# Sliding-window attention and SwiGLU: the output projection on four 64x64 TensorE tiles, with the row sums of a token group in one place

## The chip, the cores and the metric

The kernel runs on one core of a Trainium2 chip. The time is the device time of one execution in microseconds (us), the median of several runs; lower is better. A core has five engines that run their own instruction queues and wait for one another by semaphores: TensorE (PE in the profile, with its weight loads in a row of their own, PEld), VectorE (DVE), ScalarE (ACT), GpSimd (POOL) and SyncE (SP, which here only issues DMAs). Matmul results land in PSUM, which has 8 banks of 128 partitions by 512 floats.

## The reference, cut to what matters

```python
# q, k, v: (8 batches, 8 heads, 576 positions, 64)
scores = q @ k^T / sqrt(64)                      # only 0 <= i - j < 64 is kept
attn   = exp(scores - max) / sum(exp(scores - max))
x      = (attn @ v) laid out as 4608 tokens x 512
out    = (silu(x @ w_gate) * (x @ w_val)) @ w_out   # 512 -> 1536 -> 512
```

Inputs and output are float32; the kernel multiplies in bfloat16 and adds up in float32.

## The kernel before, in words

The 4608 tokens go through in nine groups of 512 (`NT` = 9, index `t`). Groups 0 to 6 and 8 are the first 512 positions of a batch each; group `LAST` = 7 gathers the last 64 positions of all eight batches. The order of all instructions is written out by hand (`tc.manual_schedule()`): each engine executes its own in the order in which the code issues them, and semaphore waits are put in where an instruction touches a tile that another engine has written or read.

For each group there are two stages.

*The attention visit.* `scores(t, w)` (L269) multiplies keys by queries for four of the eight heads, `w` = 0 or 1. Head size and window are 64, so these matmuls use 64 rows and 64 columns of the 128x128 array, and four of them, on four quarters of the array, run side by side. ACT takes the exponential out of PSUM (L282), DVE multiplies by the window's mask (L285) and adds the two blocks that share columns into `both` (L290). `sums` lets TensorE add up `both` (`totals`, L302, four 64x64x512 matmuls per `w`), and ACT makes the reciprocal of the total as exp(-log) (`log` L316, `invert` L319). `mix` (L386) multiplies the weights by the values, and `scale` (L402, DVE) multiplies the result by the reciprocal: that is `xT[t]`, the 512 tokens with the features on the partitions.

*The gate.* For each of 12 blocks `m` of 128 hidden features, `gate_value` (L448) makes g (4 matmuls of 128x128x512 with `wg`) and v (4 with `wv`) in two PSUM banks. `gate_end` lets ACT take the Silu of g (L441) and DVE multiply it by v into `hT[t][:, m]` (L442). After some blocks (`turns`) DVE transposes a quarter of the queries and keys of group t + 1 (`turn`: L207, L217), and for 3 <= t < 7 a quarter of the extra keys for `LAST` after block 8 (`turn_k`).

The output projection of group t - 1 (`project`, L457: for each of four token blocks `s` of 128, 12 matmuls of 128x128x512 over the hidden features) is put into the attention visit of group t, between scores, sums and mix, so that TensorE has work while ACT and DVE work on the softmax. `project_end` copies the PSUM result to SBUF (`os_`, L464) and SP stores it. Groups 0 and 1 meet in a visit written out by hand (L713 to L738), and the last group's projection stands at the end, its last part split in columns (`project_last`, L499). Before all that a prologue (L515 to L668) loads, casts and transposes group 0 on TensorE, and computes its attention.

PSUM: `two[0]` and `two[1]` are tiles of two banks each; `bank[4]` to `bank[7]` are tiles of one bank each. Scores and mix use `two`; g and the projection alternate between banks 4 and 5 (`out_tile`), v and the sums between banks 6 and 7 (`d_tile`); only group 1's sums use `two` (`sums_wide`).

In the loop over groups a visit reads:

```python
            set_exp()                       # ACT's table for exp and log
            scores(t, 0)
            project(t - 1, 0)
            ...
            project_part(t - 1, (1,), (o_ps,), range(5))
            scores(t, 1)
            sums(t, 0)
            project_part(t - 1, (1,), (o_ps,), range(5, 12))
            project_end(t - 1, 1, o_ps)
            project(t - 1, 2)
            sums(t, 1)
            mix_all(t)
            project(t - 1, 3)
        set_silu()                          # ACT's table for Silu
```

Loads for group t + 2 are issued by POOL (queries, keys) and SP (values) after the visit of t; nothing in their code is touched.

Of the kernel before, what the change touches and what calls it, by code (L numbers as in the profile page):

```python
# [17 lines left out]
def kernel(  # L18
# [23 lines left out]
    fsb = ctx.enter_context(tc.tile_pool(name="fsb", bufs=3))  # L42
    hpool = ctx.enter_context(tc.tile_pool(name="hpool", bufs=2))
    ps = ctx.enter_context(tc.tile_pool(name="ps", bufs=1, space=PSUM))
    two = [ps.tile([P, 2, 512], FP32, name=f"two{i}") for i in range(2)]
    bank = [two[i][:, j] for i in range(2) for j in range(2)]
    bank += [ps.tile([P, 512], FP32, name=f"one{i}")[:] for i in range(4)]

    wg = cst.tile([P, 4, DFF], BF16, name="wg")
    wv = cst.tile([P, 4, DFF], BF16, name="wv")  # L50
# [198 lines left out]
    def half(x):  # L249
        return slice(64 * x, 64 * x + 64)  # L250

    def scores(t, w):

        qT = queries[t]
        s_ps = wide(), wide()
        for j in range(8):
            if t == LAST:
                k_j = kT[t % 2 if j < 4 else 2]
                pieces = [(j, j + 1, 0, k_j, P * (j % 4) + 64),
                          (j, j + 1, 1, k_j, P * (j % 4))]  # L260
            else:
                pieces = [(j, min(8, j + 2), 0, kT[t % 2], 64 * j)]
            for lo, hi, c, src, k0 in pieces:
                for h in range(2):
                    for x in range(2):
                        slot = s_ps[h][half(x)].rearrange("r a b -> r (a b)")
                        n = hi - lo
                        o = P * j + 64 * c
                        nc.tensor.matmul(  # L269
                            slot[:, o:o + 64 * n].rearrange(  # L270
                                "r (n e y) -> r e n y", n=n, e=16
                            ),
                            src[half(h), 2 * w + x, k0:k0 + 64],
                            blocks(qT[half(h), 2 * w + x], t, lo, hi).rearrange(
                                "r e (n y) -> r e n y", n=n
                            ),
                        )
        n = 1024 if t == LAST else 960
        for h in range(2):
            E = eb[2 * w + h]  # L280
            flat = E[:].rearrange("r s z -> r (s z)")[:, 64:64 + n]
            nc.scalar.activation(  # L282
                flat, s_ps[h][:].rearrange("r a b -> r (a b)")[:, 0:n], AF.Exp, scale=0.125
            )
# [5 lines left out]
            nc.vector.tensor_add(both[:], E[:, 1:17:2], E[:, lo:lo + 15:2])  # L290
            weights[t, w, h] = E, both
# [7 lines left out]
    def totals(t, w, d):  # L299
        for h in range(2):  # L300
            for x in range(2):
                nc.tensor.matmul(  # L302
                    d[x][half(h)].rearrange("r (e j y) -> r j e y", e=16, j=8),
                    ones[half(x), 0:D],
                    weights[t, w, h][1][half(x)].rearrange("r j (e y) -> r j e y", e=16),
                )
# [11 lines left out]
    def invert(r):  # L318
        nc.scalar.activation(r, r, AF.Exp, scale=-1.0)  # L319

    def sums(t, w):
        d = d_tile(), d_tile()
        totals(t, w, d)
        for x in range(2):
            r = room(1)[:, 0]
            if t == NT - 1:
                log(r.rearrange("r (x e) -> r x e", e=16), turned(d[x]))
            else:
                log(r, d[x])
            invert(r)  # L330
            inverse[t, 2 * w + x] = r

    def sums_wide(t):
        rs = room(2), room(2)
        tiles = wide(), wide()
        for w in range(2):
            totals(t, w, (tiles[w][:, 0], tiles[w][:, 1]))
            for x in range(2):
                inverse[t, 2 * w + x] = rs[w][:, x]
        for w in range(2):  # L340
            log(rs[w], tiles[w][:])
        for w in range(2):
            invert(rs[w])

# [24 lines left out]
                    start=m == 0, stop=m == 7,  # L369
                )  # L370

    def marker(b, x):
        nc.tensor.matmul(bank[b][0:D, 0:16], ones[half(x), 0:D], ones[half(x), 0:16])

    def mix(t, w, o):
        E = [weights.pop((t, w, h))[0] for h in range(2)]
# [24 lines left out]
            r = r.rearrange("r (x e) -> r x e", e=16)  # L401
        nc.vector.tensor_mul(x, o_ps, r)  # L402

    taken = {"a": 0, "g": 0, "v": 0}

    def take(tag):
        taken[tag] += 1
        return taken[tag] % 2 ^ 1

    def wide():  # L410
        return two[take("a")]

    def d_tile():
        return bank[6 + take("v")]

    def mix_all(t):
        tiles = wide(), wide()
        for w in range(2):
            mix(t, w, (tiles[w][:, 0], tiles[w][:, 1]))
        for u in range(4):  # L420
            scale(t, u, tiles[u // 2][:, u % 2])

    def gate_one(t, m, ps, w, c):
        nc.tensor.matmul(  # L424
# [17 lines left out]
        nc.vector.tensor_mul(hT[t][:, m, :], sg[:], v_ps[:])  # L442

    def gate_value(t, m):
        pair = gate_tiles()
        for ps, w in zip(pair, (wg, wv)):
            for c in range(4):
                nc.tensor.matmul(  # L448
                    ps[:], w[:, c, P * m:P * m + P], xT[t][:, c, :],
                    start=(c == 0), stop=(c == 3),  # L450
                )
        gate_end(t, m, pair)

    def project_part(t, ss, tiles, cs):
        for c in cs:
            for s, o_ps in zip(ss, tiles):
                nc.tensor.matmul(  # L457
                    o_ps[:], hT[t][:, c, P * s:P * s + P], wo[:, c, :],
                    start=(c == 0), stop=(c == 11),
                )  # L460
# [24 lines left out]
    def out_tile():  # L485
        return bank[4 + take("g")]

    def project(t, s):
        o_ps = out_tile()
        project_part(t, (s,), (o_ps,), range(12))  # L490
        project_end(t, s, o_ps)

    def project_last(t, s):
        r0 = S * batch(t) + P * s
        os_ = fsb.tile([P, 512], FP32, name="os_", tag="os_", bufs=4)
        for f0, f1 in ((0, 384), (384, 512)):
            o_ps = out_tile()
# [149 lines left out]
    part_first((0, 1), 0, (1, 5))  # L647
    part_first((0, 1), 1, (6, 4))
    part_first((2,), 1, (2, 6, 4))
    marker(7, 1)  # L650
# [5 lines left out]
    marker(7, 0)  # L656
    for u in range(3):
        part_first((u,), 0, (0, 2, 4, 6), 6 if u < 2 else None)
    scale(0, 0, bank[aos[0]])
# [55 lines left out]
    for u in (2, 3):  # L715
        turn_q(1, u)
    scores(1, 0)
    tiles = [out_tile(), d_tile(), out_tile(), d_tile()]

    def columns(c0, c1, s0=0, s1=4):  # L720
        project_part(0, range(s0, s1), tiles[s0:s1], range(c0, c1))

    columns(0, 2, 0, 2)
    columns(0, 2, 2, 4)
    columns(2, 3)
    scores(1, 1)
    columns(3, 7)
    sums_wide(1)
    load_qk(2)
    load_halves(nc.gpsimd, vb[0], 2)  # L730
    columns(7, 9)
    columns(9, 10, 0, 2)
    mix_all(1)
    columns(9, 10, 2, 4)
    columns(10, 12, 0, 2)
    columns(10, 12, 2, 4)
    for s in range(4):
        project_end(0, s, tiles[s], on_a if s < 2 else on_v)  # L738

    for t in range(1, NT):  # L740
        if t > 1:
            set_exp()
            scores(t, 0)
            project(t - 1, 0)
            if t == 2:
                stage_v(3)
            o_ps = out_tile()
# [62 lines left out]
```

## Time and profile before

| | |
|---|---|
| median of 3 runs | 324.94 us (324.93 to 325.21) |
| span of the profiled execution, first to last instruction | 322.4 us |
| time of the profiled execution itself | not given beside its span; median less span is 2.5 us |
| PE busy | 317.1 us, 98% |
| DVE, ACT, POOL busy | 219.5, 166.8, 145.8 us |
| mean granted TensorE clock | 0.999 |
| gate matmuls (L448) | 832 of 128x128x512 |
| projection matmuls (L457, L499) | 420 of 128x128x512, 24 narrower |

How to read it: a busy time counts the time in which at least one instruction of the engine runs. Matmuls overlap, so a matmul that lasts 0.379 us by its row starts 0.216 us after the one before it. In the timeline a row stands for several equal instructions in a row: start, length, engine, line, operation, what it writes and reads, how many, and in brackets how long the engine was idle before and what ended that. Line numbers are those of the kernel before.

### The profile page before, as it was taken

To read this page: it belongs to the slowest core of one execution; us is meant where nothing else is said; L and a number is where in the kernel's file an instruction comes from. 1 tells how busy PE (TensorE), PEld (TensorE's weight loads), DVE (VectorE), ACT (ScalarE), POOL (GpSimd) and SP (SyncE) were. 2 spreads that over 40 slices of the span, in tenths; PEclk is the share of its full clock that TensorE was granted. 3 is DMA by queue.
4 is the path that set the end of the run, shared out by engine and by line. 5 is a ranking of instruction groups with operands and counts; after the bars stand their busy time and mean duration, and the time that the engine had idled before them with its cause. 6 is when DMAs were issued, how large, how long until landed. Compare 5 with 4: busy or idle time off the path is not lost.

```text
span 322.4 us, 7047 instructions
## 1 busy us (share of the span) xinstructions
PE 317.1 (98%) x2774; PEld 150.5 (47%) x2774; DVE 219.5 (68%) x349; ACT 166.8 (52%) x239; POOL 145.8 (45%) x259
## 2 busy tenths in 40 slices
PE   7999999999999999999999999999999999999995
PEld 3644444444544444444444544454444544444443
DVE  5866846597676867777688766876696586773432
ACT  5954665356633763368335833665347533773310
POOL 4955656966075795586125989462200000000000
PEclk9999999999999999999999999999999999999999
DMA  7999999999989999949903999799401400020012
GB/s 252 202 197 198 206 142 223 150 158 126 199 162 198 114 166 195 195 74 226 198 11 46 170 163 97 57 211 179 87 3 35 100 2 0 14 86 36 0 28 103
DMA packets 83521, 40.35 MB, mean 125 GB/s; under 512 B 64160, under 2 KB 78752, under 8 KB 83488
## 3 DMA queue, kind: packets, MB, share of 16 engines
q0 software_dynamic: 51488, 22.59, 58.3%
q1 hardware_dynamic: 31456, 16.79, 21.0%
q10 hardware_dynamic: 544, 0.52, 0.5%
q8 instruction: 21, 0.34, 0.4%
q14 instruction: 12, 0.10, 0.1%
HBM read 53.02 MB, written 9.44 MB: 194 GB/s over the span
## 4 chain that ended last, share of the span: by engine, by line
PE 95%; DMA 2%; DVE 1%; SPq 1%; issue 0%; DVEq 0%
PE one L448 56%; PE one L457 29%; PE two L269 3%; PE two L386 2%; DMA k_f<-in_k_dram 2%; PE one L424 2%; PE one L302 1%; PE one L499 1%; SPq L77 1%; PE two L424 1%; DVE kT L198 0%; PE two L702 0%; PE one L351 0%; DVE qT L573 0%; PE two L302 0%
## 5 line engine op out<-in xcount | busy, mean ns | idle before, releaser
L441 ACT ACTIVATE sg<-one 128x512 f32<-128x512 f32 x107 | 63.9, 597 | 113.6 <-PE one L448 86.7
L442 DVE TENSOR_TENSOR hT<-sg,one 128x512 bf16<-128x512 f32 x107 | 74.2, 694 | 61.9 <-PE one L448 57.8
L448 PE MATMUL one<-xT,wg 128*128 128x512 bf16 x416 | 106.8, 379 | 0.0
L448 PE MATMUL one<-xT,wv 128*128 128x512 bf16 x416 | 106.8, 379 | 0.0
L457 PE MATMUL one<-wo,hT 128*128 128x512 bf16 x420 | 95.2, 380 | 0.0
L126 POOL DMA_DIRECT2D k_s<-in_k_dram x112 | 60.8, 552 | 29.0 <-DMA q_s<-in_q_dram 21.8
L448 PEld LDWEIGHTS <-wv 128*128 128x128 bf16 x416 | 40.7, 98 | 49.1
L448 PEld LDWEIGHTS <-wg 128*128 128x128 bf16 x416 | 40.5, 98 | 48.8
L457 PEld LDWEIGHTS <-hT 128*128 128x128 bf16 x420 | 39.0, 98 | 46.7 <-issue 2.0
L282 ACT ACTIVATE eb<-two 128x960 bf16<-128x960 f32 (+1 forms) x32 | 29.5, 975 | 15.1 <-PE two L269 15.0
L217 DVE STREAM_TRANSPOSE kT<-k_s 128x512 bf16<-128x512 bf16 x28 | 36.1, 1289 | 0.0
L285 DVE TENSOR_TENSOR eb<-eb,mask 128x960 bf16<-128x960 bf16 (+1 forms) x32 | 21.1, 658 | 11.5 <-ACT eb L282 11.5
L402 DVE TENSOR_TENSOR xT<-two,r 128x512 bf16<-128x512 f32 x34 | 21.8, 686 | 6.4 <-PE two L386 4.8
L177 POOL CAST vb<-v_f 128x512 bf16<-128x512 f32 x20 | 11.5, 619 | 30.3 <-DMA v_f<-in_v_dram 19.4
L319 ACT ACTIVATE r<-r 128x512 f32<-128x512 f32 (+1 forms) x34 | 22.2, 657 | 1.0
L207 DVE STREAM_TRANSPOSE qT<-q_s 128x512 bf16<-128x512 bf16 x32 | 22.3, 701 | 0.1
L316 ACT ACTIVATE r<-one 128x512 f32<-128x512 f32 x31 | 18.3, 590 | 4.7 <-PE one L302 4.7
L91 POOL DMA_DIRECT2D q_s<-in_q_dram x24 | 13.1, 566 | 4.3 <-DVE qT L207 4.2
L290 DVE TENSOR_TENSOR both<-eb 128x512 bf16<-128x512 bf16 x32 | 13.6, 425 | 1.1
L152 POOL DMA_DIRECT2D vb<-in_v_dram x16 | 11.1, 718 | 4.6 <-DMA wo<-in_moe_w_out_dram 3.4
L507 ACT ACT_TABLE_LOAD x9 | 11.5, 1283 | 2.0 <-issue 1.9
L98 POOL DMA_DIRECT2D q_s<-in_q_dram x16 | 8.6, 627 | 7.5 <-DVE qT L207 7.5
(128 smaller groups left out, 198.4 us busy)
## 6 DMA issues: line engine op xcount, KB each, us to landing
k_s<-in_k_dram POOLq DMA_DIRECT2D x112, 56.0 KB, 4.8
q_s<-in_q_dram POOLq DMA_DIRECT2D x24, 248.0 KB, 5.9
v_f<-in_v_dram SPq DMA_DIRECT2D x40, 128.0 KB
wg<-in_moe_w_gate_dram POOLq DMA_DIRECT2D x5, 256.0 KB, 8.4
wv<-in_moe_w_val_dram POOLq DMA_DIRECT2D x5, 256.0 KB, 9.4
q_f<-in_q_dram SPq DMA_DIRECT2D x4, 256.0 KB
wo<-in_moe_w_out_dram POOLq DMA_DIRECT2D x2, 512.0 KB, 9.9
vb<-in_v_dram POOLq DMA_DIRECT2D x16, 64.0 KB, 4.6
```

What stands on the lines that cost most here:

```text
L126: nc.gpsimd.dma_start(k_s[p0:p0 + 32, g, :, 0:w], k[b, a:H:2, s:s + P].rearrange("u (r e) d -> r u (e d)", e=4) [:, :, 32 * c:32 * c + w],)
L207: nc.vector.transpose(queries[t][:, u, :].rearrange("r (e x) -> r e x", e=16), staged[t][0][:, u].rearrange("r (e d) -> r e d", d=D)[:, :, ...
L217: nc.vector.transpose(dst[:, u, :].rearrange("r (g x e) -> r g e x", g=4, e=4), k_s[:, :, u].rearrange("r g (e d) -> r g e d", d=D)[:, :, ...
L282: nc.scalar.activation(flat, s_ps[h][:].rearrange("r a b -> r (a b)")[:, 0:n], AF.Exp, scale=0.125)
L285: nc.vector.tensor_mul(flat, flat, mask[:].rearrange("r j c e y -> r (j c e y)")[:, 0:n])
L316: nc.scalar.activation(r, d_ps, AF.Ln)
L319: nc.scalar.activation(r, r, AF.Exp, scale=-1.0)
L402: nc.vector.tensor_mul(x, o_ps, r)
L441: nc.scalar.activation(sg[:], g_ps[:], AF.Silu)
L442: nc.vector.tensor_mul(hT[t][:, m, :], sg[:], v_ps[:])
L448: nc.tensor.matmul(ps[:], w[:, c, P * m:P * m + P], xT[t][:, c, :], start=(c == 0), stop=(c == 3),)
L457: nc.tensor.matmul(o_ps[:], hT[t][:, c, P * s:P * s + P], wo[:, c, :], start=(c == 0), stop=(c == 11),)
```

## The change

The PSUM tiles become four tiles of two banks; bank numbers stay, so banks 4 and 5 are the halves of `two[2]`, banks 6 and 7 of `two[3]`. In the visits the projection runs as `project_quads`: each 128x128x512 matmul becomes four of 64x64x512, one for each quarter of the array. The two halves of the contraction (x) work on different token blocks at the same time (`s` and `s + 2`), since they write different banks, and a second pass with `back=1` gives each block its other half. `sums(t)` makes both parts in one place, in `two[0]` and `two[1]`, as `sums_wide` did. The gate of t >= 1 takes its g and v as the two halves of `two[3]` and `two[2]` in turn (for block 0 of group 1, of `two[0]`); scores, sums and mix always use `two[0]` and `two[1]`. The copies out of PSUM are divided between DVE and ACT. The gate of t = 0 keeps `out_tile` and `d_tile`.

```diff
-    two = [ps.tile([P, 2, 512], FP32, name=f"two{i}") for i in range(2)]
-    bank = [two[i][:, j] for i in range(2) for j in range(2)]
-    bank += [ps.tile([P, 512], FP32, name=f"one{i}")[:] for i in range(4)]
+    two = [ps.tile([P, 2, 512], FP32, name=f"two{i}") for i in range(4)]
+    bank = [two[i][:, j] for i in range(4) for j in range(2)]
...
     def gate_value(t, m):
-        pair = gate_tiles()
+        if t == 0:
+            pair = gate_tiles()
+        else:
+            i = 0 if (t, m) == (1, 0) else 3 - m % 2
+            pair = two[i][:, 0], two[i][:, 1]
...
+    def project_quads(t, tiles, cs, g, back):
+
         for c in cs:
-            for s, o_ps in zip(ss, tiles):
-                nc.tensor.matmul(
-                    o_ps[:], hT[t][:, c, P * s:P * s + P], wo[:, c, :],
-                    start=(c == 0), stop=(c == 11),
-                )
+            for y in range(2):
+                for x in range(2):
+                    s = g + 2 * (x ^ back)
+                    r0 = P * s + 64 * y
+                    nc.tensor.matmul(
+                        tiles[s][half(y)], hT[t][half(x), c, r0:r0 + 64],
+                        wo[half(x), c, :],
+                        start=not back and c == 0, stop=bool(back) and c == 11,
+                    )
...
+    tiles = [bank[5], bank[4], bank[7], bank[6]]
+    project_quads(0, tiles, range(4), 0, 0)
+    project_quads(0, tiles, range(4), 1, 0)
+    project_quads(0, tiles, range(4, 6), 0, 0)
     scores(1, 1)
-    columns(3, 7)
-    sums_wide(1)
+    project_quads(0, tiles, range(4, 8), 1, 0)
+    project_quads(0, tiles, range(6, 12), 0, 0)
+    for x in range(2):
+        marker(two[x][0:D, 1, 448:464], x)
+    project_quads(0, tiles, range(8, 12), 1, 0)
+    for x in range(2):
+        on_a(seen[:], two[x][0:D, 1, 448:449])
+    sums(1)
...
+    tiles = [bank[6], bank[4], bank[7], bank[5]]
     for t in range(1, NT):
         if t > 1:
             set_exp()
             scores(t, 0)
-            project(t - 1, 0)
+            project_quads(t - 1, tiles, range(12), 0, 0)
             if t == 2:
                 stage_v(3)
-            o_ps = out_tile()
-            project_part(t - 1, (1,), (o_ps,), range(5))
             scores(t, 1)
-            sums(t, 0)
-            project_part(t - 1, (1,), (o_ps,), range(5, 12))
-            project_end(t - 1, 1, o_ps)
-            project(t - 1, 2)
-            sums(t, 1)
+            project_quads(t - 1, tiles, range(12), 1, 0)
+            sums(t)
+            project_quads(t - 1, tiles, range(12), 0, 1)
             mix_all(t)
-            project(t - 1, 3)
+            project_end(t - 1, 0, tiles[0])
+            scale_all(t)
+            project_end(t - 1, 2, tiles[2], on_a)
+            project_quads(t - 1, tiles, range(12), 1, 1)
         set_silu()
+        if t > 1:
+            project_end(t - 1, 1, tiles[1], on_a)
+            project_end(t - 1, 3, tiles[3], on_v)
...
     for s in range(3):
-        project(NT - 1, s)
+        project(NT - 1, s, (bank[6], bank[7], bank[0])[s])
     project_last(NT - 1, 3)
```

`project_last` takes `bank[1]` and `bank[2]` for its two column parts.

More of the change, by code (lines that the diff above doesn't have):

```diff
@@ L254, in scores @@
         qT = queries[t]
-        s_ps = wide(), wide()
+        s_ps = two[0], two[1]
         for j in range(8):
@@ L319, in invert, with sums @@
         nc.scalar.activation(r, r, AF.Exp, scale=-1.0)
[L321 to L333, printed above, removed]
+    def sums(t):
         rs = room(2), room(2)
-        tiles = wide(), wide()
         for w in range(2):
-            totals(t, w, (tiles[w][:, 0], tiles[w][:, 1]))
+            totals(t, w, (two[w][:, 0], two[w][:, 1]))
             for x in range(2):
@@ L340, in sums_wide @@
         for w in range(2):
-            log(rs[w], tiles[w][:])
+            if t == NT - 1:
+                log(
+                    rs[w].rearrange("r b (x e) -> r b x e", e=16),
+                    two[w][:].rearrange("r b (e x) -> r b x e", e=16),
+                )
+            else:
+                log(rs[w], two[w][:])
         for w in range(2):
@@ L370, in joined_first, with marker @@
                 )
-    def marker(b, x):
-        nc.tensor.matmul(bank[b][0:D, 0:16], ones[half(x), 0:D], ones[half(x), 0:16])
+    def marker(to, x):
+        nc.tensor.matmul(to, ones[half(x), 0:D], ones[half(x), 0:16])
     def mix(t, w, o):
@@ L402, in scale @@
         nc.vector.tensor_mul(x, o_ps, r)
-    taken = {"a": 0, "g": 0, "v": 0}
+    taken = {"g": 0, "v": 0}
     def take(tag):
@@ L408, in take @@
         return taken[tag] % 2 ^ 1
-    def wide():
-        return two[take("a")]
     def d_tile():
@@ L416, in mix_all, with scale_all @@
     def mix_all(t):
-        tiles = wide(), wide()
         for w in range(2):
-            mix(t, w, (tiles[w][:, 0], tiles[w][:, 1]))
+            mix(t, w, (two[w][:, 0], two[w][:, 1]))
+    def scale_all(t):
         for u in range(4):
-            scale(t, u, tiles[u // 2][:, u % 2])
+            scale(t, u, two[u // 2][:, u % 2])
     def gate_one(t, m, ps, w, c):
@@ L444, in gate_value @@
     def gate_value(t, m):
-        pair = gate_tiles()
+        if t == 0:
+            pair = gate_tiles()
+        else:
+            i = 0 if (t, m) == (1, 0) else 3 - m % 2
+            pair = two[i][:, 0], two[i][:, 1]
         for ps, w in zip(pair, (wg, wv)):
@@ L452, in gate_value @@
         gate_end(t, m, pair)
-    def project_part(t, ss, tiles, cs):
+    def project_quads(t, tiles, cs, g, back):
         for c in cs:
-            for s, o_ps in zip(ss, tiles):
-                nc.tensor.matmul(
-                    o_ps[:], hT[t][:, c, P * s:P * s + P], wo[:, c, :],
-                    start=(c == 0), stop=(c == 11),
-                )
+            for y in range(2):
[6 more added lines that the diff above has]
+                        start=not back and c == 0, stop=bool(back) and c == 11,
+                    )
     def project_end(t, s, o_ps, copy=nc.vector.tensor_copy):
@@ L486, in out_tile, with project @@
         return bank[4 + take("g")]
-    def project(t, s):
-        o_ps = out_tile()
-        project_part(t, (s,), (o_ps,), range(12))
+    def project(t, s, o_ps):
+        for c in range(12):
+            nc.tensor.matmul(
+                o_ps, hT[t][:, c, P * s:P * s + P], wo[:, c, :],
+                start=(c == 0), stop=(c == 11),
+            )
         project_end(t, s, o_ps)
@@ L495, in project_last @@
         os_ = fsb.tile([P, 512], FP32, name="os_", tag="os_", bufs=4)
-        for f0, f1 in ((0, 384), (384, 512)):
-            o_ps = out_tile()
+        for f0, f1, o_ps in ((0, 384, bank[1]), (384, 512, bank[2])):
             for c in range(12):
@@ L649 @@
     part_first((2,), 1, (2, 6, 4))
-    marker(7, 1)
+    marker(bank[7][0:D, 0:16], 1)
     on_v(seen[:], bank[7][0:D, 0:1])
@@ L655 @@
     part_first((0, 1), 0, (7,))
-    marker(7, 0)
+    marker(bank[7][0:D, 0:16], 0)
     for u in range(3):
@@ L717 @@
     scores(1, 0)
[L718 to L725, printed above, removed]
-    scores(1, 1)
-    columns(3, 7)
-    sums_wide(1)
+    tiles = [bank[5], bank[4], bank[7], bank[6]]
+    project_quads(0, tiles, range(4), 0, 0)
+    project_quads(0, tiles, range(4), 1, 0)
+    project_quads(0, tiles, range(4, 6), 0, 0)
+    scores(1, 1)
+    project_quads(0, tiles, range(4, 8), 1, 0)
[6 more added lines that the diff above has]
+    sums(1)
     load_qk(2)
     load_halves(nc.gpsimd, vb[0], 2)
-    columns(7, 9)
-    columns(9, 10, 0, 2)
+    project_quads(0, tiles, range(12), 0, 1)
     mix_all(1)
[L734 to L738, printed above, removed]
+    project_end(0, 0, tiles[0])
+    scale_all(1)
+    project_end(0, 2, tiles[2], on_a)
+    project_quads(0, tiles, range(12), 1, 1)
+    project_end(0, 3, tiles[3], on_a)
+    project_end(0, 1, tiles[1], on_v)
+    tiles = [bank[6], bank[4], bank[7], bank[5]]
     for t in range(1, NT):
@@ L743 @@
             scores(t, 0)
-            project(t - 1, 0)
+            project_quads(t - 1, tiles, range(12), 0, 0)
             if t == 2:
                 stage_v(3)
-            o_ps = out_tile()
-            project_part(t - 1, (1,), (o_ps,), range(5))
             scores(t, 1)
-            sums(t, 0)
-            project_part(t - 1, (1,), (o_ps,), range(5, 12))
-            project_end(t - 1, 1, o_ps)
-            project(t - 1, 2)
-            sums(t, 1)
+            project_quads(t - 1, tiles, range(12), 1, 0)
+            sums(t)
+            project_quads(t - 1, tiles, range(12), 0, 1)
             mix_all(t)
-            project(t - 1, 3)
+            project_end(t - 1, 0, tiles[0])
+            scale_all(t)
+            project_end(t - 1, 2, tiles[2], on_a)
+            project_quads(t - 1, tiles, range(12), 1, 1)
         set_silu()
+        if t > 1:
+            project_end(t - 1, 1, tiles[1], on_a)
+            project_end(t - 1, 3, tiles[3], on_v)
         if t + 1 == LAST:
```

## The prediction

> **What bounds the kernel now.** I read the page first: which engine is full, and what the chain that ended last is made of.
>
> ```profile
> PE 317.1 (98%) x2774; PEld 150.5 (47%) x2774; DVE 219.5 (68%) x349; ACT 166.8 (52%) x239; POOL 145.8 (45%) x259
> PE 95%; DMA 2%; DVE 1%; SPq 1%; issue 0%; DVEq 0%
> ```
>
> TensorE is busy 98% of the span and 95% of the last chain: a matmul taken away, or a nanosecond of TensorE waiting, moves the end. So I ask two things: what TensorE saves, and whether it must now wait. Second, the table of stretches, cut at a token group's gate phase and at the next attention visit (t = 3):
>
> ```profile
> 84.01:104.82 20.81, 20.81 (x97) 9.27 (x95) 13.75 (x19) 7.73 (x14) 11.92 (x22) 1.00 1.06 181
> 104.82:117.91 13.09, 13.09 (x186) 6.59 (x186) 10.50 (x18) 10.25 (x14) 11.01 (x22) 1.00 1.05 138
> ```
>
> The columns are us, then busy time of PE, PEld, DVE, ACT, POOL. TensorE never stops in either; in the visit ACT is busy 10.25 of 13.09 us and DVE 10.50, so there the other engines are close behind. Third, the timeline of that visit:
>
> ```profile
> 104.07 0.60 ACT L441 ACTIVATE sg<-one 128x512 f32<-128x512 f32 x1 [1.13 <-PE one L448]
> 104.68 1.28 ACT L507 ACT_TABLE_LOAD   x1
> 104.82 0.62 PE L269 MATMUL two<-qT,kT 64*64 64x128 bf16 x32
> 105.37 3.84 PE L457 MATMUL one<-wo,hT 128*128 128x512 bf16 x17
> 105.98 1.83 ACT L282 ACTIVATE eb<-two 128x960 bf16<-128x960 f32 x2
> 109.15 0.62 PE L269 MATMUL two<-qT,kT 64*64 64x128 bf16 x32
> 109.60 0.39 PE L302 MATMUL one<-both,ones 64*64 64x512 bf16 x4
> 109.92 4.27 PE L457 MATMUL one<-wo,hT 128*128 128x512 bf16 x19
> 112.53 0.42 DVE L290 TENSOR_TENSOR both<-eb 128x512 bf16<-128x512 bf16 x1
> ```
>
> The last Silu of the gate starts at 104.07, when only its g half is done (the v half runs to 104.73); table load and two exponentials follow on ACT and end at 107.81. TensorE comes back for the second scores at 109.15, 1.3 us later. That reserve is what the change spends. Fourth, the timeline of the gate round a transposition on DVE:
>
> ```profile
> 160.44 1.03 PE L448 MATMUL one<-xT,wg 128*128 128x512 bf16 x4
> 160.71 0.69 DVE L442 TENSOR_TENSOR hT<-sg,one 128x512 bf16<-128x512 f32 x1 [1.04 <-PE one L448]
> 161.31 0.70 DVE L207 STREAM_TRANSPOSE qT<-q_s 128x512 bf16<-128x512 bf16 x1
> 161.94 1.29 DVE L217 STREAM_TRANSPOSE kT<-k_s 128x512 bf16<-128x512 bf16 x1
> 163.03 0.71 DVE L442 TENSOR_TENSOR hT<-sg,one 128x512 bf16<-128x512 f32 x1
> ```
>
> A multiply holds DVE 0.60 us (160.71 to 161.31), the two transposes 1.72 (to 163.03).
>
> **What the change saves.** Single TensorE starts in the trace: 128x512 matmuls follow each other at 0.216 us; going to 64x64 tiles the step is 0.309 and the first group of four takes 0.024 more; going back, again 0.093 and 0.010 more. A pair of switches costs 0.22 us. A visit from t = 2 on has three pairs, the first visit (t = 1) four; afterwards each has one. Saved: 7 x 0.44 + 0.66 = 3.8 us. The projection's 48 matmuls become 192 of 64x64x512, in 48 groups of four. No such stream is in the trace. Lower end: 0.216 a group, the step out of the sums (L302, 64x64x512) less the switch; 512 columns pass at no quicker rate anywhere. Upper end: 0.240, the first L302 group after a switch, or +0.024 x 48 x 8 visits = +9.2 us. I take 0.216: the 64x64x128 groups of L386 and L269 also pay the 0.024 only in their first group and then run at 0.056, each with four weight loads. The loads hide too: 64*64 loads last 0.105 us each by row, overlapped.
>
> **Where the change adds waits.** PSUM was four single-bank tiles and two double ones; it becomes four double ones. In the built program's order with its waits, a reader or writer of one half now waits for the other half. From t = 1 the Silu counts TensorE up to the last v matmul (before: the last g matmul), and the g matmuls of block m+2 count DVE up to the multiply of block m (before: only the Silu; the v matmuls waited for the multiply, 0.86 us later). I follow this through, with E the end of a block's matmuls (1.728 us a block), ACT 0.20 after TensorE (next group 102.14, Silu 102.34), Silu 0.60, DVE 0.03 later (exponential to mask multiply), multiply 0.69 to 0.71, TensorE 0.05 after DVE (kT copy end 6.20, scores 6.25).
>
> *Gate, plain block:* 0.20 + 0.60 + 0.03 + 0.69 + 0.05 = 1.57 after E; the buffer is wanted at E + 1.73. Reserve 0.15, no stall. *Gate, block with transposes:* multiply m starts E + 0.83, transposes E + 1.43, multiply m+1 at E + 3.16, its end and hand-over E + 3.92; block m+3 wanted it at E + 3.46. Stall **0.47**. Transposes after blocks 1, 4 and 7 stall; after block 10 no block follows. The extra transpose at block 8 (t = 3 to 6) fits. So 1.40 us for each t = 2 to 7: 8.4. At t = 1 (6, 7, 9, 10) two transposes queue up: 0.47 + 0.60 = 1.1.
>
> *Visit, t = 2 to 8*, from E: Silu 0.20 to 0.80, table load to 2.09, exponentials 2.11 to 3.94. TensorE: switch and scores to 0.54, 12 groups to 3.14; the second scores wait for the second exponential until 3.99 (**stall 0.85**); end 4.44, 12 groups to 7.03. The sums, now in one visit, need the last `both`: exponential start 4.65 + 3.14 (109.81 to 112.95 above) + 0.05 = 7.85, **stall 0.58**; end 8.07. 12 groups 10.66; mix 0.85, 11.51 (the logarithms are through by 9.4); 12 groups 14.10; switch 14.20. Before: 13.18 (104.73 to 117.91). Each visit +1.02, though two switch pairs are saved: 7.1 in all. Behind them ACT and DVE copy the four results one after the other, ending 15.6; the second gate block wants that buffer at 15.9, so these hide.
>
> *Prologue.* The copies of qT and kT out of two halves of one buffer now wait for all eight transposes and for each other: kT copy 6.82 instead of 6.20, so the first scores +0.6. The next row sums wait for the next kT copy, in the neighbouring half (8.95 instead of 7.80, +1.15); a warming matmul waits for ACT's logarithm beside it (10.04 instead of 8.47, +1.57), and all behind it is on this chain; the fourth scores wait for their kT copy (+1.73); the fourth row sums wait for the third logarithm (16.0): the first gate matmul goes from 14.37 to 16.7, the first blocks end 20.5 instead of 18.1. **+2.4.** *Gate, t = 0.* Buffers pair g with g and v with v of neighbouring blocks, so v of a block waits for the multiply before it: 0.15 at blocks 6, 7, 9 and 10 (before 8 and 11 TensorE's own 0.57 of transposes covers it), 0.77 and 0.95 at 4 and 5, where DVE builds the mask for 2.07 us; g of block 2 waits 0.20 for a Silu. **+2.5.** *First visit.* The first quads need the buffer that the last multiply reads, 0.47 late; the last quads need the buffer that ACT copies behind logarithms and inverses of 1.0 us each (wanted 49.83, free 50.77 in the shifted time: 0.94); the sums just fit; 0.66 of switches is saved, two marker pairs add 0.05. **+0.8.** *Tail.* The last projections use neighbouring halves, so twice TensorE waits 0.20 + 0.69 + 0.05 for DVE's copy: **+1.9.**
>
> **Sum:** 2.4 + 2.5 + 0.8 + 1.1 + 7.1 + 8.4 + 1.9 = +24.2 us. POOL's and SP's instructions keep their order of loads; the four output DMAs of each s move 2 to 6 us later in the visit and their buffers are reused 34 us on, so they cost nothing. The span is 322.4 us; I take the 2.5 us between it and the median of 324.94 to stay, since no time of the profiled execution itself is shown. **349.1 us.** Hand-overs 0.03 shorter or 0.04 longer at some 43 stalls give -1.3 to +1.7, and I trust the prologue to 1: own range 346.5 to 352; with the upper end for a quad group, 358.
>
> **Rivals.**
> *The transposes hide* (0.05): if DVE were free 0.47 us sooner, gates and their 9.5 us go: 339.6. Against it: all 28 kT transposes have the 1.29 us.
> *No reserve in the plain block* (0.06): it decides if the three hand-overs together take over 0.15 us more; at 0.15 beyond that, some 80 blocks lose 12 us: 361. Against it: the hand-overs repeat to 0.01 us in every block.
> *Weight loads not hidden* (0.03): in a quad the second pair loads rows that a running matmul uses. Were those two loads of 0.105 us exposed, 384 groups lose 81 us: 430. Against it: L386 has this very order (both row halves, then the other columns) and steps 0.056 us a group. [...]
> *Not slower* (0.05): the saved switches stand alone, 324.94 - 3.8 = 321.2. The place is the 0.44 us saved per visit against that visit's wait; it decides if ACT's chain from the last Silu to the second exponential ended before 3.14 and the last `both` before 7.4, and the gate's g half were free at the Silu. Against it: the built waits name the multiply, and 2.09 - 0.80 of table load cannot shrink.
>
> **How the numbers follow.** Forecast 0.81. The range 343 to 358 takes in both ends of the unknown group and, below, 3.5 us for waits of the prologue and the first token group that I may have counted twice; it leaves out the four rivals, 0.19. A measurement of this kernel tells about 0.2% from no change. Faster is the last rival nearly whole, 0.04; a tie within it 0.01; slower 0.95.
>
> **What would show it.** Right: PE below 95% busy; idle TensorE before the g matmuls of blocks 4, 7, 10, released by DVE's multiply, 0.47 each; before the second scores 0.85, released by ACT; before the sums 0.58, by DVE; Silu starts 0.20 after the v half; quad groups at 0.216. Wrong: quads at 0.24 or more, or gate blocks without gaps at the transposes, or all of them with gaps.

## The result, and the profile after

The changed kernel takes **350.47 us** (median of four runs, 350.39 to 350.66) where the kernel before takes 324.94 (324.92 to 325.21): 1.079 times as long, 95% interval 1.078 to 1.081. 349.1 was forecast. The two lines of the page that were read first before, now after:

```profile
PE 323.7 (93%) x3928; PEld 171.4 (49%) x3928; DVE 210.4 (60%) x335; ACT 170.1 (49%) x227; POOL 146.7 (42%) x259
PE 35%; DMA 21%; DVE 18%; POOL 10%; ACT 10%; issue 4%; DVEq 0%; SPq 0%; POOLq 0%
```

TensorE fell from 98% to 93% of a longer span. Its share of the last chain fell from 95% to 35%: other engines now end what TensorE waits for. The table of stretches of the changed kernel, a gate phase (t = 3) and the visit behind it (t = 4):

```profile
130.38:152.60 22.22, 21.32 (x98) 9.28 (x98) 14.59 (x20) 7.15 (x12) 2.33 (x5) 1.00 0.49 97
152.60:166.70 14.10, 13.25 (x329) 9.23 (x329) 9.28 (x16) 11.24 (x12) 9.92 (x19) 1.00 0.86 126
```

The gate was 20.81 us with 20.81 of TensorE, the visit 13.09 with 13.09. The visit's timeline shows both of its waits:

```profile
152.70 0.60 ACT L431 ACTIVATE sg<-two 128x512 f32<-128x512 f32 x1 [1.14 <-PE two L442]
153.32 1.28 ACT L508 ACT_TABLE_LOAD   x1
154.61 1.83 ACT L281 ACTIVATE eb<-two 128x960 bf16<-128x960 f32 x2
156.50 0.59 PE L268 MATMUL two<-qT,kT 64*64 64x128 bf16 x29 [0.62 <-ACT eb L281]
157.14 1.83 ACT L281 ACTIVATE eb<-two 128x960 bf16<-128x960 f32 x2 [0.69 <-PE two L268]
159.49 0.62 PE L301 MATMUL two<-both,ones 64*64 64x512 bf16 x6
160.34 0.40 PE L301 MATMUL two<-both,ones 64*64 64x512 bf16 x2 [0.23 <-DVE both L289]
```

The last Silu starts 0.10 us after the visit begins (152.70 against 152.60). In the kernel before it started 0.75 us ahead of the visit (104.07 against 104.82): now it waits for the v half too. Table load and exponentials follow unbroken, and the second scores stand behind them. Two of those scores got through at 155.64, the rest came at 156.50: 0.86 us from start to start, of which the view counts 0.62 as idle, because it lets a matmul's modelled end run on. And the gate round a transposition:

```profile
135.28 0.70 DVE L206 STREAM_TRANSPOSE qT<-q_s 128x512 bf16<-128x512 bf16 x1
135.91 1.28 DVE L216 STREAM_TRANSPOSE kT<-k_s 128x512 bf16<-128x512 bf16 x1
137.00 0.71 DVE L432 TENSOR_TENSOR hT<-sg,two 128x512 bf16<-128x512 f32 x1
137.76 1.02 PE L442 MATMUL two<-xT,wg 128*128 128x512 bf16 x4 [0.30 <-DVE hT L432]
```

The multiply starts behind both transposes, and the g matmuls start 0.76 us after it. The four v matmuls ahead of them start at 136.44, so the g matmuls were due at 137.30: 0.46 us is lost, three times in each such gate.

The whole profiled execution, cut at the first scores of each visit and at the first gate matmul behind it (start to start, us):

| stretch | before | after | forecast | measured |
|---|---|---|---|---|
| start to the first visit | 36.80 | 41.75 | +4.9 | +4.95 |
| visit t = 1 | 13.32 | 14.38 | +0.8 | +1.06 |
| gate t = 1 | 20.81 | 21.88 | +1.1 | +1.07 |
| visit t = 2 | 13.08 | 15.16 | +1.02 | **+2.08** |
| visit t = 3 | 13.08 | 15.01 | +1.02 | **+1.93** |
| visits t = 4, 5, 6, 8, each | 13.08 | 14.10 | +1.02 | +1.02 |
| visit t = 7 | 13.61 | 14.68 | +1.02 | +1.07 |
| gates t = 2 to 7, each | 20.81 | 22.21 | +1.40 | +1.40 |
| last gate to the end | 34.51 | 36.41 | +1.9 | +1.9 |
| span | 322.4 | 349.0 | +24.2 | +26.6 |

Most terms fit to some hundredths. Three visits (t = 1, 2 and 3) don't, and they are what the experiments had to explain beside the theory itself. How close the first row comes is in part luck: in four other profiled executions with the same prologue the first visit starts at 42.11 to 43.84 us instead of 41.75.

### The profile page after: what moved, and what is told of

Its sections match the earlier page's. It is cut to its first block, busy times and chain, and to the rows that moved or that the text cites. A ratio compares the mean times of both kernels' runs of the same rounds, so it can differ in the third digit from the quotient of the medians.

```text
span 349.0 us, 9221 instructions
## 1 busy us (share of the span) xinstructions
PE 323.7 (93%) x3928; PEld 171.4 (49%) x3928; DVE 210.4 (60%) x335; ACT 170.1 (49%) x227; POOL 146.7 (42%) x259
## 4 chain that ended last, share of the span: by engine, by line
PE 35%; DMA 21%; DVE 18%; POOL 10%; ACT 10%; issue 4%; DVEq 0%; SPq 0%; POOLq 0%
PE two L442 22%; PE two L455 7%; DMA q_s<-in_q_dram 6%; DVE kT L216 6%; DVE hT L432 5%; DMA wv<-in_moe_w_val_dram 5%; ACT eb L281 4%; ACT sg L431 4%; POOL k_s L125 4%; DMA k_s<-in_k_dram 4%; DVE qT L206 3%; DMA wo<-in_moe_w_out_dram 3%; POOL q_s L97 2%; ACT L508 2%; DVE eb L284 2%
## 5 line engine op out<-in xcount | busy, mean ns | idle before, releaser
L431 ACT ACTIVATE sg<-two 128x512 f32<-128x512 f32 x108 | 64.4, 597 | 130.6 <-PE two L442 128.1
L432 DVE TENSOR_TENSOR hT<-sg,two 128x512 bf16<-128x512 f32 x108 | 74.8, 693 | 74.7 <-ACT sg L431 64.3
L442 PE MATMUL two<-xT,wg 128*128 128x512 bf16 x416 | 106.8, 379 | 6.2 <-DVE hT L432 6.2
L442 PE MATMUL two<-xT,wv 128*128 128x512 bf16 x416 | 106.7, 379 | 1.4 <-DVE hT L432 1.4
L455 PE MATMUL two<-wo,hT 64*64 64x512 bf16 x1536 | 92.3, 376 | 0.7 <-issue 0.6
L455 PEld LDWEIGHTS <-hT 64*64 64x64 bf16 x1536 | 55.6, 107 | 22.4 <-issue 1.4
L315 ACT ACTIVATE r<-two 128x1024 f32<-128x1024 f32 (+1 forms) x20 | 18.0, 936 | 9.2 <-PE two L301 8.4
L318 ACT ACTIVATE r<-r 128x1024 f32<-128x1024 f32 (+1 forms) x20 | 18.5, 970 | 0.1
L268 PE MATMUL two<-qT,kT 64*64 64x128 bf16 (+1 forms) x576 | 11.9, 210 | 4.4 <-ACT eb L281 4.4
L268 PEld LDWEIGHTS <-kT 64*64 64x64 bf16 x576 | 9.7, 105 | 10.2 <-issue 8.7
```

Of the source, the lines that this page charges most:

```text
L268: nc.tensor.matmul(slot[:, o:o + 64 * n].rearrange("r (n e y) -> r e n y", n=n, e=16), src[half(h), 2 * w + x, k0:k0 + 64], blocks(qT[half ...
L431: nc.scalar.activation(sg[:], g_ps[:], AF.Silu)
L442: nc.tensor.matmul(ps[:], w[:, c, P * m:P * m + P], xT[t][:, c, :], start=(c == 0), stop=(c == 3),)
L455: nc.tensor.matmul(tiles[s][half(y)], hT[t][half(x), c, r0:r0 + 64], wo[half(x), c, :], start=not back and c == 0, stop=bool(back) and c = ...
```

## The experiments

A *quad group*, or quad, is the four 64x64x512 matmuls that replace one 128x128x512 matmul. Theory: the merged PSUM tiles make halves wait for each other, and this costs all that was lost. Rivals: the quads themselves, or the row sums made in one place, hold TensorE up. Since the first 14 us of one program differ by up to 2 us between executions (last section), I compare the stretches from the first visit on wherever they decide.

**Single tiles again.** Only the declaration and its use change:

```diff
-    two = [... for i in range(4)]
-    bank = [two[i][:, j] for i in range(4) for j in range(2)]
+    two = [... for i in range(2)]
+    bank = [two[i][:, j] for i in range(2) for j in range(2)]
+    bank += [ps.tile([P, 512], FP32, name=f"one{i}")[:] for i in range(4)]
...
-            pair = two[i][:, 0], two[i][:, 1]
+            pair = bank[2 * i], bank[2 * i + 1]
```

> The changed kernel with the tile declaration of before: two double PSUM tiles and four single ones; gate pairs take the same banks as in the changed kernel, and quads, order and the sums in one visit stay. My theory (waits are counted per tile, so halves of a merged tile wait for each other): the first gate phase starts 2.4 us earlier, the gate of t = 0 loses 2.5, the gates of t = 1 to 7 lose 1.1 and 1.40 each and have 20.81 us again, the tail loses 1.9: 16 to 17 us in all. In a visit the last Silu starts 0.86 us earlier, so the second scores need not wait; then TensorE reaches the sums earlier and waits about 0.8 us for the last both: a visit 13.2 to 13.3 us instead of 14.10. Total 326 to 328 us. Rival 1, the quads or the sums in one visit make the gates wait: the gate phases stay at 22.2 us, total about 350. Rival 2, the merging costs in the gates only: about 341.

Measured 330.81 us (329.73 to 330.93; 1.017 times before, 1.014 to 1.020). All gates from t = 1 to 7 take 20.82 us, the first visit starts at 37.07, and visits t = 2, 4, 5, 6 and 8 take 13.24, as expected. The table of stretches for the gate t = 3:

```profile
122.38:143.20 20.82, 20.82 (x97) 9.32 (x96) 15.08 (x21) 7.89 (x14) 5.76 (x11) 1.00 0.61 112
```

Both rivals fall. The total is 2.8 us above the range, mainly for three reasons: the first visit waits 1.2 us for `wo` to land, which it now reaches earlier; the tail keeps 0.96 us of its wait, since two of the last projections still use the halves of one double tile; and the visit t = 3 takes 16.23. The timeline of that visit has these rows:

```profile
109.00 2.82 DVE L290 TENSOR_TENSOR both<-eb 128x512 bf16<-128x512 bf16 x1
109.24 2.28 POOL L177 CAST vb<-v_f 128x512 bf16<-128x512 f32 x4
```

An add that takes 0.42 us elsewhere takes 2.82 beside POOL's cast of v, and the last row sums start 1.93 us later in the visit than at t = 4. This is the same quarrel as in the visit t = 2 of the changed kernel, below. Another 0.88 us of this visit is a stop of TensorE that no row explains (see the last experiment).

**The wait in the gates, with tiles merged.** The kT transposes move one block on, DVE's work stays:

```diff
-                turn(t + 1, turns.index(m))
-            if m == 8 and 3 <= t < 7:
+                turn_q(t + 1, turns.index(m))
+            ks = turns if t == 1 else (2, 5, 8, 11)
+            if m in ks and t + 1 < NT:
+                turn_k(kT[(t + 1) % 2], staged[t + 1][1], ks.index(m))
+            if m == 9 and 3 <= t < 7:
```

> The changed kernel with merged tiles and all, only that from t = 2 the kT transposition (1.29 us of DVE) is issued one gate block later than the qT transposition (0.43), the extra one of t = 3 to 6 after block 9 instead of 8. DVE does the same work. My theory (the g matmuls wait for a multiply that is late by a queue of 0.60 + 1.72 us): with 0.60 + 1.29 us in one block the reserve of 0.15 just covers it, the gaps at blocks 4, 7 and 10 go, gates t = 2 to 7 have 20.8 us, total 350.5 - 8.4 = 342.1. Rival, the gap is the price of the later Silu or of DVE's sum of work in a gate: gates stay at 22.2 us, total 350.5; or the gaps only move to other blocks, the same total.

Measured 342.64 us (341.67 to 344.11; 1.055, 1.051 to 1.059). The table of stretches for the gate t = 3:

```profile
130.56:151.39 20.83, 20.83 (x99) 9.30 (x98) 14.63 (x20) 7.16 (x12) 3.54 (x7) 1.00 0.54 106
```

DVE is as busy as with the gaps (14.63 against 14.59 us), the Silu as late, and every gate from t = 2 on has 20.82 us. So the gap comes from the queue ahead of one multiply: with 0.60 + 1.72 us in it TensorE waits, and with 0.60 + 1.29 the reserve of 0.15 us holds. Neither DVE's sum of work nor the later Silu by itself costs a gate anything.

**The load that came too early.** In the visit t = 2 of the changed kernel, DVE and POOL show:

```profile
81.67 3.09 POOL L176 CAST vb<-v_f 128x512 bf16<-128x512 f32 x4
82.48 1.06 DVE L284 TENSOR_TENSOR eb<-eb,mask 128x960 bf16<-128x960 bf16 x1
84.21 1.06 DVE L284 TENSOR_TENSOR eb<-eb,mask 128x960 bf16<-128x960 bf16 x1
```

In the kernel before, the cast stood at 88.00, behind the visit. SP issues `stage_v(3)` in program order; there the output DMAs of the projection's first part were ahead of it. SP's queue before, and one row of it after:

```profile
75.86 1.80 SPq L483 DMA_DIRECT2D out_dram<-os__1104  x4
77.70 6.42 SPq L152 DMA_DIRECT2D v_f<-in_v_dram  x8
```

```profile
59.29 8.13 SPq L151 DMA_DIRECT2D v_f<-in_v_dram  x8
```

The change moves those output DMAs behind the mix, so nothing holds the load, and it goes out at 59.29 instead of 77.70. The experiment puts it behind the moved output DMAs:

```diff
-            if t == 2:
-                stage_v(3)
             scores(t, 1)
...
             project_end(t - 1, 2, tiles[2], on_a)
+            if t == 2:
+                stage_v(3)
```

> The changed kernel with the loads of v for t = 3 issued on SP behind the two output copies of the visit t = 2, as late as they came before the change, in place of ahead of the second scores. Theory: the visit t = 2 is 1.05 us longer than t = 4 since these loads no longer stood behind an output DMA, landed 18 us earlier, and POOL's cast of v ran beside the mask multiplies, which took 1.06 us instead of 0.65. Expected: cast after the visit, multiplies 0.65, visit t = 2 14.10 us, total 349.4. Rival, the multiplies are slow there for another reason (DMA traffic, POOL's own descriptors): visit stays at 15.1, total 350.5.

The visit takes 14.11 us, its multiplies 0.66, 0.65, 0.66 and 0.65, and the cast comes at 104.42, in the gate. The median says less (350.44 us, 348.27 to 350.73, where 349.4 was expected): the profiled execution lost 2 us ahead of the first visit (43.84 against 41.75), and from there on took 305.06 us against 307.20. The rival of DMA traffic isn't excluded yet: that visit moved only 41 GB/s where the slow one moved 125.

**Whole matmuls in the changed order.**

```diff
         for c in cs:
-            for y in range(2):
-                for x in range(2):
-                    s = g + 2 * (x ^ back)
-                    r0 = P * s + 64 * y
-                    nc.tensor.matmul(
-                        tiles[s][half(y)], hT[t][half(x), c, r0:r0 + 64],
...
+            s = g + 2 * back
+            nc.tensor.matmul(
+                tiles[s], hT[t][:, c, P * s:P * s + P], wo[:, c, :],
+                start=c == 0, stop=c == 11,
+            )
```

> The changed kernel with whole 128x128 matmuls of 128x512 in place of the quads (one matmul for each group of four, the same tiles, in the same places; a token group is now finished in one stretch). Theory: a quad group costs as much as a matmul, and what the quads save is mode switches of 0.09 to 0.12 us; the two ahead of the second scores and the sums fall into waits, the others show: about +0.2 us a visit, total 352 to 352.6. Rival 1, quads are slower than matmuls by 0.024 a group: total 350.5 + 2 - 9 = 343. Rival 2, the quads save nothing since all switches fall into waits: 350.5.

Measured 351.82 us (350.94 to 352.65), just under the range that was expected. The visits t = 3 to 6 and 8 take 14.34 us, against 14.10 with quads; t = 2, with its cast, takes 15.11. So a quad group costs no more than its matmul, and in the changed kernel the quads earn 0.24 us a visit: the other switches that they save would have fallen into waits.

**A better order on single tiles.** Four quad groups move ahead of the sums, and the rest is spread round the two mixes. The smaller edits that the expectation names, on the logarithms, the loads, the first visit and the last projections, are not shown:

```diff
             project_quads(t - 1, tiles, range(12), 1, 0)
+            marker(two[0][0:D, 1, 448:464], 1)
+            project_quads(t - 1, tiles, range(4), 0, 1)
             sums(t)
-            project_quads(t - 1, tiles, range(12), 0, 1)
-            mix_all(t)
+            project_quads(t - 1, tiles, range(4, 12), 0, 1)
+            mix(t, 0, (two[0][:, 0], two[0][:, 1]))
             project_end(t - 1, 0, tiles[0])
+            project_quads(t - 1, tiles, range(4), 1, 1)
+            mix(t, 1, (two[1][:, 0], two[1][:, 1]))
             scale_all(t)
...
-            project_quads(t - 1, tiles, range(12), 1, 1)
+            project_quads(t - 1, tiles, range(4, 12), 1, 1)
```

> The kernel with single tiles of the first experiment, and in each visit from t = 2: four quad groups more ahead of the sums (behind a marker matmul that waits for the first of the second exponentials, so that they are ordered behind the groups that wrote the same banks), eight between sums and the first mix, four between the two mixes, eight behind; each logarithm followed by its inverse; the loads of v for t = 3 behind the output copies, the extra loads of k one token group later, so that POOL's casts of v fall into the gates; in the first visit two columns of quads behind the second scores; the last projections on tiles that nobody reads. My theory: nothing waits in a visit but the gate's first matmul for DVE's last scaling, about 0.1: visits of 12.75 us against 13.24 with single tiles alone and 13.08 before; no multiply or add of DVE above 0.75 us in a visit, so t = 3 loses its 3 us; gates 20.82, last part 34.5 instead of 35.5. Total of the sections 320 to 322, or 0.2 to 0.7% below before (322.4). Rival 1: the quads' saved switches are worth nothing once the waits are gone: visits of 13.08 or more, total 322.4 or above. Rival 2: the 3 us of t = 3 are not DVE beside POOL's cast and stay: 324.

> The same kernel with whole 128x128 matmuls in place of the quads. Theory: with the waits gone the mode switches show: four more pairs in a visit from t = 2, of 0.22 us each, some in the wait for DVE's scaling: visits of 13.4 to 13.6 us, total 5 to 6 us above the one with quads. Rival: a quad group takes longer than the matmul it replaces by as much as a switch saves: the same visit length as with quads.

With quads 325.27 us (324.24 to 326.21; 1.002, 1.000 to 1.003), with whole matmuls 331.10 (330.60 to 332.51; 1.020, 1.017 to 1.022). The plain visits take 12.75 us as worked out, and 13.77 with whole matmuls: in this order, without waits, the quads are worth 1.02 us a visit. Against the order of before, which has fewer switches (visits of 13.08), it is 0.33. The expected 13.4 to 13.6 was too low, since I had forgotten the pair of switches round the marker, a matmul of 16 columns that only carries a wait: five more pairs than with quads, 0.20 us each. Rival 1 falls. The total with quads missed its range by three visits: t = 1 (14.36 us), where the quads reach columns of `wo` that land late; t = 3 (13.52), with a stop that no row explains; and t = 4 (13.67), into which a cast now falls.

**Whole matmuls in the first visit, a cast once more moved.**

```diff
-    project_quads(0, tiles, range(4), 0, 0)
...
+    columns(0, 2, 0, 2)
+    columns(0, 2, 2, 4)
+    columns(2, 3)
     scores(1, 1)
...
-        elif t + 1 < NT and t > 1:
+        elif t + 1 < NT and t > 1 and t != 3:
             cast_v(t + 1)
...
         if t == 2:
+            cast_v(4)
             k_l = load_k(
```

> The reordered kernel with two things put right that its trace shows: the first visit (t = 1) has whole matmuls in the order of before, since the quads there come to columns of wo that have not landed (14.36 us with quads, 13.32 before); and POOL casts the v of t = 4 ahead of the extra loads of k, so that no cast falls into a visit (at t = 4 it had lengthened the mask multiplies from 0.65 to 1.06 us and the visit from 12.75 to 13.67). Theory: first visit 13.3, visits t = 2 to 8 12.75 (t = 7 13.1), no DVE row of a visit above 0.75 us, gates 20.82: from the first visit on 283.2 us against 285.6 before, total 0.5 to 0.7% below before, less up to 0.8 us if TensorE once more waits for nothing that the trace shows. Rival: the casts only move on to another visit, or the quads' order meets wo in t = 2 as well: no faster than before.

Measured 323.53 us (322.62 to 325.05) beside 324.55 for before: 0.997, 0.994 to 0.999. This is faster than before by more than the measurement is uncertain, though less than the 0.5 to 0.7% that was expected. The first visit has 13.32, and t = 2, 3, 5, 6 and 8 have 12.75. But a cast still falls into the visit t = 4, which takes 14.22 where it took 13.67: I had moved the second cast in POOL's order, and the one in this visit is the third, of v for t = 5. The visit t = 4 has:

```profile
142.73 2.28 POOL L177 CAST vb<-v_f 128x512 bf16<-128x512 f32 x4
143.03 2.50 DVE L285 TENSOR_TENSOR eb<-eb,mask 128x960 bf16<-128x960 bf16 x1 [0.38 <-ACT eb L282]
```

The visit t = 7 takes 13.72 where 13.1 was expected; 0.38 of the difference is a stop in its second mix.

**No cast on POOL.** ACT, idle 1.13 us in each gate block, takes it. (The next load of v, issued behind these casts, is not shown.)

```diff
-        elif t + 1 < NT and t > 1 and t != 3:
-            cast_v(t + 1)
...
             gate_value(t, m)
+            if m in (5, 6, 8, 9) and t > 1 and t + 1 < NT and t + 1 != LAST:
+                i = 2 * (5, 6, 8, 9).index(m)
+                on_a(vb[(t + 1) % 2][:, i:i + 2], staged[t + 1, "v"][:, i:i + 2])
```

> The kernel before this with the four casts of v a token group taken from POOL and given to ACT, behind the Silu of gate blocks 5, 6, 8 and 9 (ACT is idle 1.13 us in each block; a cast of this size takes it about 0.61), and the next load of v issued behind them. Theory: DVE's multiplies and adds were slow only beside POOL's cast, so with no cast on POOL the visit t = 4 goes from 14.22 to 12.75 us and all DVE rows of visits are 0.66 and 0.43; gates stay at 20.82, as a cast ends before the next Silu can start; total 1.5 us less, 320.3 to 321 in the sections, 0.6 to 1.0% below before. Rival 1: t = 4 is slow for its DMA traffic or POOL's descriptors: it stays above 14. Rival 2: the casts delay Silu and multiply: gates above 20.9.

Measured 323.35 us (323.00 to 323.80) beside 324.92: 0.996, 0.994 to 0.997, the fastest of all. The gates stay at 20.82. The visit t = 4:

```profile
139.70:152.44 12.74, 12.74 (x330) 8.33 (x329) 8.75 (x15) 10.08 (x11) 8.00 (x15) 1.00 1.15 189
```

It moves 189 GB/s where the slow visit t = 2 of the changed kernel moved 125, with 8.00 us of POOL's DMA issues, and no DVE row in it is long. So neither traffic nor descriptors slow DVE, the cast does. The gain, 0.4%, is below the 0.6 to 1.0% that I expected: t = 3 has 13.60 us, 0.85 too much, again by a stop that no row explains.

**The stops that no row explains.** In the changed kernel TensorE stood still twice with no releaser named:

```profile
53.14 0.46 PE L378 MATMUL two<-eb,vb 64*64 64x128 bf16 x21 [0.91 <-issue]
129.00 1.45 PE L455 MATMUL two<-wo,hT 64*64 64x512 bf16 x21 [0.57 <-issue]
```

A fetch of instructions (a DMA queue of its own, 16 KB each; 30 here and 21 before, for 2308 more matmuls and weight loads, or by estimate some 256 to a fetch) begins 2.31 and 2.34 us ahead of these two ends; the stops at t = 3 of the kernel with single tiles and of the last kernel end 2.33 and 2.31 us behind such a start, the one of the kernel with moved transposes 2.48, that of the reordered kernel 2.99. To test it, the changed kernel ran again unaltered and with its TensorE program shifted by small matmuls at the start:

```diff
-    keep_warm(6)
+    keep_warm(4)
+    for _ in range(32):
+        nc.tensor.matmul(warm[0:D, 0:16], ones[:, 0:D], ones[:, 0:16])
```

> The changed kernel again, unaltered, beside three copies whose TensorE program is shifted. In its first profile TensorE stood still twice for nothing that the trace names (0.91 us in the first mix, 0.57 in the last quads of t = 3). Theory: it waits for a fetch of its own program, 16 KB at a time; each such gap ends 2.3 us after a fetch begins, and quads make these fetches frequent (30 where there were 21). Then gaps here stand behind fetches in the same places or nowhere. Rival: the gaps come from the place itself (the density of small matmuls, a semaphore): then they stand in the same places in all four kernels.

> 32 matmuls of 16 columns take the place of two warming matmuls at the start, where TensorE waits for loads: 30 matmuls, or 60 with their weight loads, a quarter of a fetch, further on in the program. Theory: fetches shift by a quarter, and a gap, if there is one, stands at another place and still ends 2.3 us after a fetch begins. Rival: same places as without the shift.

> 64 small matmuls for four warming ones: half a fetch further on. Theory and rival as for the quarter.

> 96 small matmuls for six warming ones: three quarters of a fetch further on. Theory and rival as for the quarter.

One run each: 350.79, 351.96, 352.63 and 354.20 us, beside 326.20 for before. Unaltered, the stops are back in the very same places, ahead of the last 21 matmuls of their groups:

```profile
53.08 0.47 PE L378 MATMUL two<-eb,vb 64*64 64x128 bf16 x21 [0.49 <-issue]
128.79 1.45 PE L455 MATMUL two<-wo,hT 64*64 64x512 bf16 x21 [0.44 <-issue]
```

In all three shifted kernels neither row shows a stop, and t = 3 takes 14.10 or 14.11 us where the unaltered one takes 14.88. (The length of t = 1 tells nothing here: it is 14.05 or 14.06 in all four, since in the unaltered kernel the stop covers a wait for ACT's copy.) At t = 7, which takes 14.68 with 64, three of them stop: the unaltered one and that with 32 in the mix (15.02 and 15.05), and the one with 96 in the last quads (15.30), ending 2.64, 2.42 and 2.62 behind the start of a fetch. This speaks for the fetch and against a semaphore of that place. It isn't proof: the shifted kernels also start 2 to 5 us later, and the kernel with the later load, which has the unshifted TensorE program but also started 2 us late, had no stop either. What delays a fetch stays open. The size doesn't: about 1.2 us of the 26.6.

The shifted kernels also bear on the cast. With 64 small matmuls the load of v goes out just as early (63.14), but the cast runs at the very start of the visit t = 2, which begins at 81.88, and is over when the first mask multiply starts:

```profile
82.40 2.29 POOL L176 CAST vb<-v_f 128x512 bf16<-128x512 f32 x4
84.90 0.66 DVE L284 TENSOR_TENSOR eb<-eb,mask 128x960 bf16<-128x960 bf16 x1 [0.96 <-ACT eb L281]
```

That visit takes 14.10 us. With 96 the cast meets one multiply (1.07 us), the waits for ACT's exponentials cover that, and the visit takes 14.11. So the early load by itself costs nothing; it costs 1 us where the cast happens to fall on several multiplies and adds.

## Why the prediction was right, point by point

- *Merged tiles wait for the other half:* right, shown by undoing the merge alone, which takes 20 us of the 25.5 away.
- *Gates 1.40 and 1.1:* right, 1.40 and 1.07; the moved transposes show that the place of one 1.29 us instruction decides. The rival of hidden transposes fails because DVE was not free sooner; the rival without reserve fails because the reserve of 0.15 held in every plain block.
- *Visits 1.02:* right to 0.01 at t = 4, 5, 6 and 8, with both parts: 0.86 at the second scores, and in the sums the last pair starts at 160.34, where the pair before it (159.73) would have let it start at 159.76: 0.58.
- *Quad group 0.216 us:* right: at t = 4 the first 12 groups take 2.59 us from start to start (153.05 to 155.64). Neither the 0.240 of the upper end nor exposed weight loads show: 48 groups take as long as 48 whole matmuls. The loads, 0.107 us each by row, are hidden in this order of quads, as they are in the 0.056 us groups that the prediction held against that rival.
- *Prologue, gate t = 0, tail:* right in sum, 4.95 for 4.9 and 1.9 for 1.9, and undoing the merge brings the first visit back to 37.07. The 0.05 is luck, since the start moves by up to 2 us between executions. Inside the gate t = 0, v of block 5 waited 0.61 and not 0.95, and that of block 9 0.57 and not 0.15.
- *First visit +0.8:* in this execution the wait for ACT's copy was covered by the stop in the mix, which cost more. In the kernel with the later load, which has no stop there, the last quads wait for that copy, and the visit has 14.05, or +0.73.
- **The step that failed:** "POOL's and SP's instructions keep their order of loads; [...] so they cost nothing". The order is kept; what stood ahead of `stage_v(3)` is not. The output DMAs went, the load ran 18 us ahead, POOL's cast fell among the mask multiplies and adds, and the visit t = 2 lost 1.06 us more. I counted what moved instructions do to their own queue, not whom they had been holding back.
- *Not in the sum at all:* the stops without a releaser, +0.3 at t = 1 and +0.9 at t = 3.
- *Between span and time:* I carried over 2.5 us; the changed kernel has 350.66 for its span of 349.0, 1.7 us, and an execution of before with a span of 322.4 took 324.14, the same 1.7. I had set a median beside the span of another, quicker execution. That error of 0.8 hid a third of the 2.4 that the sum lacked, so that 349.1 came so near to 350.47 is in part luck.

## What to carry to other kernels

When buffers are merged, list for each half who reads it, and ask who of them is now waited for by a writer of the other half; then follow that wait to the engine's longest queue, which here was one transposition ahead of a multiply. A saving on a full engine pays only if what feeds it still ends earlier: kernels with these quads lose 8%, or gain 0.4%, by the tiles that the quads are put on, the order around them and the engine that casts v. And when a DMA moves, look at what had been queued behind it, since that now comes early, to an engine that may be in the way of another.

## What the runs showed of the hardware

*POOL's cast holds DVE up.* A DVE multiply or add with both operands in SBUF took 1.06 instead of 0.65 (changed kernel, t = 2), 2.82 instead of 0.42 (single tiles, t = 3) and 2.50 instead of 0.65 us (the kernel with a cast once more moved, t = 4) beside a cast on POOL. The casts lose as well: the four at 81.67 took 3.09 us, the four at 111.94 took 2.29. A gate multiply, which has one operand in PSUM, kept its 0.69 us at 112.20 beside these latter. In the kernel before two took 0.71 and 0.69 us at 163.03 and 164.16, beside the four casts that take 2.30 us from 162.90. Why DVE is slow beside a cast is not shown.

*The clock at the start.* Kernels with the same prologue differ by up to 2 us in the start of the first visit (41.75 to 43.84). In the profiled execution of the kernel with the later load the granted clock was 0.53 and 0.50 between 7.5 and 14.4 us:

```profile
7.50:11.00 3.50, 2.83 (x39) 1.42 (x31) 2.35 (x5) 2.34 (x4) 3.50 (x6) 0.53 1.42 253
```

Matmuls that take 0.41 us take 0.64 there. Its first transposes had waited 0.66 us for ACT's cast of the loaded data, where they waited 0.33 in the changed kernel's first profile, at clock 1.00. That the longer wait brought the lower clock on is not shown, since no run here varied the wait by itself. Two other late starts go with slow matmuls too. Their profiles and the changed kernel's first one begin with 512-column matmuls of 0.63 us. In the changed kernel such matmuls take 0.40 from 5.42 on, in the kernel with whole matmuls (first visit at 42.94) only from 9.09 on, and in the one with moved transposes (43.77) only from 13.48 on, although the tables of these two show the clock as 1.00 throughout.
